# Attention and a gated MLP on one core: the moves of turned probabilities issued on ScalarE's queue instead of SyncE's, with the order of operations rewritten

## The chip, the cores and the metric

One core of one Trainium2 chip runs the whole program. The metric is the time of one execution on the device in microseconds (us), as the median of several runs.

## The reference

Causal attention of 4 batches, 12 heads, 448 positions and head size 64, then a gated MLP over the 1792 tokens of 768 features (12 heads x 64), all in float32:

```python
scores = scale * np.matmul(q, k.transpose(0, 1, 3, 2))
scores = np.where(mask, -1000000000.0, scores)
scores = scores - np.max(scores, axis=-1, keepdims=True)
attn = np.exp(scores)
attn = attn / (np.sum(attn, axis=-1, keepdims=True) + 1e-09)
x = np.matmul(attn, v)               # then (B, H, S, D) -> (B * S, H * D)
gate = 1.0 / (1.0 + np.exp(-(x @ w_gate)))
val = x @ w_val
out = gate * val @ w_out             # 768 -> 1536 -> 768
```

## The kernel before

**The work.** A pair is two heads of one batch; there are 24, six to a batch. A unit is one batch's 448 tokens. Two units go through the MLP one after the other (`unit_items`, then `first_out`); the last two go through it together (`pair_items`) by a scheme of seven products of half-sized blocks. Each product in full precision is three matmuls of rounded halves: high x high, high x low and low x high (`triple` at L756, `mm` at L972). For these, ScalarE makes the high half of a weight tile (L666) and GpSimd or VectorE the low half (L668).

**The weights.** They arrive as words of 64 bits. A load (L642, issued by SyncE) brings a tile into the buffer `room`; ScalarE (L646) and VectorE (L648, L650) convert it to float32. A `keep` (L656) writes it to the chip's memory, and later fetches (L660) bring it back.

**Attention.** Pairs 0 to 5 are done first, in narrow steps. Pairs 6 to 23 run "wide", between about 60 and 390 us, spread among the MLP's products. For a wide pair SyncE loads the raw operands (L358, L363) and V (L369). TensorE computes the scores (L475) and VectorE adds the mask and takes the extremes (L498). ScalarE takes exponentials with their sums (L505), VectorE the reciprocals (L514, L516), and GpSimd scales the probabilities (L526). Then `shift` turns the pair. GpSimd clears a corner of the turned buffer (L537), which waits until an earlier pair's moves have read that buffer. VectorE transposes blocks of 32 x 32 in eight instructions (L541, L544). **Four moves** (L550) each copy 32 partitions of the turned buffer, `tb` or from pair 18 on a part of `room`, into one column range of `pt`, so that blocks that lay on four groups of partitions come to lie on one. Each move waits for all eight transposes and the clearing. `wpv` then multiplies with V: a burst of 40 matmul records (L566), which needs all four moves. ScalarE rounds the result (L443) and VectorE takes the rest (L444), as features of the MLP.

**The order.** Every instruction of the program (or small group, as three matmuls, or a burst) is one operation, given to the planner by `plan.op` with its engine, a cost in us and, as `extra`, the time until its result can be used. Operations are numbered in the order of these calls, 0 to 3069. The order in which they are written into the engines' queues is not computed in the kernel: `TABLE` lists all 3070 numbers, and `Plan.order` only asserts that it holds every number once and that no operation stands ahead of one that it depends on. An engine runs its own operations in the order of that list, each waiting for its inputs. A DMA is issued by the engine that it is listed for, in the same queue as that engine's other work. All DMAs of the kernel before are issued by SyncE ("SP" in the plan, "SPq" in the profile).

```python
full = [(tb, "zero", "end", *[(z, i) for z in range(2) for i in range(3)], (0, 3))]
for a in range(4):
    plan.op("SP", dma(32 * 4 * WC * 4), lambda a=a: nc.sync.dma_start(
        out=pt.t[:, a * WC:a * WC + WC], in_=at_()[32 * a:32 * a + 32]), full, [(pt, a)], extra=4.2)
```

Of the kernel before, what the change touches and what calls it, by code (L numbers as in the profile page):

```python
# [40 lines left out]
WC = 512  # L41
# [248 lines left out]
def kernel(  # L290
# [7 lines left out]
    nc = tc.nc  # L298
    plan = Plan()
# [10 lines left out]
    dma = lambda b: b / 355e3 + 0.03  # L310
# [219 lines left out]
    def shift(n):  # L530
# [18 lines left out]
        for a in range(4):  # L549
            plan.op("SP", dma(32 * 4 * WC * 4), lambda a=a: nc.sync.dma_start(  # L550
                out=pt.t[:, a * WC:a * WC + WC], in_=at_()[32 * a:32 * a + 32]), full, [(pt, a)], extra=4.2)
# [705 lines left out]
```

## Time and profile before

| | |
|---|---|
| median of 3 runs | 640.65 us (638.57 to 642.12) |
| the profiled execution | 641.33 us, its span 639.4 us |
| mean granted clock of TensorE | 0.995 |
| busy: TensorE, VectorE, ScalarE, GpSimd | 610.3, 459.6, 335.3, 310.9 us |
| DMA: hardware queue that SyncE issues on | 131.36 MB, 62.4% of 16 engines' span |
| moves at L550 | 48 from `tb`, 24 from `room`: 18 pairs x 4, 256 KB each |

The span runs from the first to the last instruction of one execution; the time of the run also has what lies around it. Busy times are of the engines' instructions; a queue's time in issuing a DMA or in waiting isn't counted as busy. A number in brackets at the end of a timeline row is the engine's idle time before that instruction, with what ended it.

### The profile page before, as it was taken

The page shows a single profiled execution, that of the slowest core. Times are in us where ns is not written, and L with a number is a line of the kernel's source. Part 1 is how long each engine was busy: PE and PEld are TensorE (multiplying, and loading weights), DVE is VectorE, ACT ScalarE, POOL GpSimd, SP SyncE. Part 2 cuts the span into 40 slices and gives each one's busy share as a digit, 9 for nine tenths or more (in the row PEclk, how much of TensorE's full clock was granted, in tenths as well). Part 3 has the DMA queues.
Part 4 walks back from the last instruction along what each step waited for, and adds up shares of the span by engine and source line. Part 5 has one row for each costly group of instructions (what it writes and reads, how often), then busy time and mean ns, then how long its engine had stood idle before and what let it go on. Part 6 is the DMA issues. An engine that isn't in the chain of part 4 may idle for free.

```text
span 639.4 us, 11811 instructions
## 1 busy us (share of the span) xinstructions
PE 610.3 (95%) x4128; PEld 527.2 (82%) x4128; DVE 459.6 (72%) x1109; ACT 335.3 (52%) x760; POOL 310.9 (49%) x349
## 2 busy tenths in 40 slices
PE   7999998989999999999899899999999999999997
PEld 4567887868998788888688698889999999899996
DVE  4879887988786766678868768864546366978862
ACT  6788656645543737556537544643343343465630
POOL 3660323241555666667567784574566557410120
PEclk9999999999999999999899999999999999999999
DMA  6489999998998899994675595222422322424512
GB/s 236 115 321 342 288 353 303 310 310 265 371 304 314 293 316 364 310 332 138 195 208 160 156 278 190 89 78 96 139 75 74 126 74 74 132 90 129 186 46 86
DMA packets 51034, 132.09 MB, mean 207 GB/s; under 512 B 5664, under 2 KB 12320, under 8 KB 50976
## 3 DMA queue, kind: packets, MB, share of 16 engines
q1 hardware_dynamic: 50976, 131.36, 62.4%
q8 instruction: 32, 0.52, 0.3%
q14 instruction: 26, 0.21, 0.1%
HBM read 89.26 MB, written 23.20 MB: 176 GB/s over the span
## 4 chain that ended last, share of the span: by engine, by line
PE 45%; DMA 19%; DVE 16%; ACT 7%; issue 5%; POOL 4%; SPq 3%; DVEq 0%; ACTq 0%; POOLq 0%
PE m L972 18%; PE s L972 10%; PE m L756 7%; PE t L972 5%; DMA room<-in_wp_dram 4%; DMA wr<-wdram 4%; DVE sm L498 3%; DMA sum<-wd 3%; POOL sm L526 2%; ACT sm L505 2%; DMA out_dram<-gt 2%; DMA pt<-room 2%; PE m L566 2%; SPq L550 2%; PE t L401 2%
## 5 line engine op out<-in xcount | busy, mean ns | idle before, releaser
L526 POOL TENSOR_SCALAR sm<-sm,r 128x384 f32<-128x384 f32 (+3 forms) x165 | 96.9, 606 | 105.7 <-DVE r L516 75.8
L756 PE MATMUL m<-xh,wh 128*128 128x448 f32 x342 | 128.6, 376 | 3.6 <-DVE r L514 1.9
L756 PE MATMUL m<-xh,wl 128*128 128x448 f32 x342 | 126.5, 370 | 2.3 <-POOL wl L668 1.7
L756 PE MATMUL m<-xl,wh 128*128 128x448 f32 x342 | 125.6, 367 | 0.0
L944 POOL TENSOR_TENSOR wl<-room,wh 128x384 fp32r<-128x384 f32 x84 | 91.2, 1107 | 64.5 <-ACT wh L943 63.1
L505 ACT ACTIVATE sm<-sm,mn 128x384 f32<-128x384 f32 (+3 forms) x168 | 88.0, 526 | 39.1 <-DVE mn L498 32.0
L668 POOL TENSOR_TENSOR wl<-wr,wh 128x768 fp32r<-128x768 f32 x46 | 88.3, 1924 | 34.6 <-ACT wh L666 34.3
L943 ACT CAST wh<-room 128x384 fp32r<-128x384 f32 x84 | 40.8, 511 | 71.1 <-DVE room L953 25.0
L756 PEld LDWEIGHTS m<-xh,wh 128*128 128x128 f32 x342 | 64.7, 189 | 12.8 <-issue 2.7
L666 ACT CAST wh<-wr 128x768 fp32r<-128x768 f32 x57 | 47.3, 831 | 52.9 <-DMA wr<-wdram 24.6
L756 PEld LDWEIGHTS m<-xh,wl 128*128 128x128 f32 x342 | 64.6, 189 | 9.9 <-POOL wl L668 3.5
L756 PEld LDWEIGHTS m<-xl,wh 128*128 128x128 f32 x342 | 64.8, 190 | 4.9
L541 DVE STREAM_TRANSPOSE tb<-sm 128x384 f32<-128x384 f32 (+2 forms) x84 | 34.9, 442 | 25.6 <-POOL sm L526 20.6
L498 DVE CUSTOM_DVE_ANT_0 sm<-s,mask 128x128 f32<-128x128 f32 (+3 forms) x108 | 41.9, 400 | 8.2 <-PE s L475 8.1
L972 PE MATMUL m<-pt,wh 128*128 128x448 f32 x150 | 44.8, 367 | 1.5 <-DVE xl L725 1.1
L475 PE MATMUL s<-raw 64*64 64x128 f32 (+3 forms) x432 | 40.6, 405 | 5.9 <-DMA raw<-in_qkt_dram 3.6
L566 PEld LDWEIGHTS m<-pt,vr 128*64 128x64 f32 x720 | 34.8, 141 | 12.2 <-issue 8.7
L725 DVE TENSOR_TENSOR xl<-m,xh 128x448 f32<-128x448 f32 x30 | 18.5, 621 | 35.8 <-PE m L972 35.5
L566 PE MATMUL m<-pt,vr 128*64 128x128 f32 (+1 forms) x720 | 37.1, 260 | 5.8 <-DMA pt<-room 3.4
L756 PE MATMUL m<-ob,wh 128*128 128x448 f32 x120 | 35.1, 372 | 2.9 <-DVE ob L735 1.5
L972 PE MATMUL m<-sm,wh 128*128 128x448 f32 x126 | 36.8, 365 | 0.0
L953 DVE TENSOR_TENSOR room<-room 128x384 f32<-128x384 f32 x48 | 30.2, 632 | 7.2 <-POOL wl L944 6.6
(207 smaller groups left out, 1357.0 us busy)
## 6 DMA issues: line engine op xcount, KB each, us to landing
room<-in_wp_dram SPq DMA_DIRECT2D x36, 768.0 KB, 7.4
room<-wdram SPq DMA_DIRECT2D x36, 384.0 KB, 3.6
pt<-tb SPq DMA_DIRECT2D x48, 256.0 KB, 4.9
raw<-in_qkt_dram SPq DMA_DIRECT2D x23, 448.0 KB, 6.9
wr<-wdram SPq DMA_DIRECT2D x24, 384.0 KB, 5.6
sum<-wd SPq DMA_DIRECT2D x21, 384.0 KB, 5.3
wr<-sum SPq DMA_DIRECT2D x21, 384.0 KB, 5.5
room<-sum SPq DMA_DIRECT2D x21, 384.0 KB, 3.7
```

The costliest lines, as they stand in the source:

```text
L475: nc.tensor.matmul(out=sp[z].t[c:c + 64, o:o + ne], lhsT=q, rhs=k)
L498: plan.op("DVE", dve(n), lambda z=z, i=i, sp=sp, sm=sm, n=n, o=o, f=f, lo=lo, to=to, first=first: nc.vector.tensor_tensor_reduce(out=sm.t[ ...
L505: plan.op("ACT", act(ne, 0, 1) + 0.09, lambda z=z, sm=sm, i=i, ne=ne, off=off: nc.scalar.activation(out=sm.t[:, off:off + ne], in_=sm.t[:, ...
L526: plan.op("PL", 0.24 + w / 1200, lambda sm=sm, e=e, o=o, w=w, z=z: nc.gpsimd.tensor_scalar(out=sm.t[:, o:o + w], in0=sm.t[:, o:o + w], sca ...
L541: plan.op("DVE", dve(128 * c) + 0.03, lambda sm=sm, i=i, o=o, c=c, at=at: nc.vector.transpose(out=tv()[:, :, at:at + 32 * c].rearrange("p ...
L566: nc.tensor.matmul(out=vp.t[64 * z:64 * z + 64, i * WQ:i * WQ + rows(i)], lhsT=v.t[:, c, z], rhs=src, start=(c == 0), stop=(c == i))
L666: plan.op("ACT", act(768), lambda: nc.scalar.copy(hi_.t, t.t), [(t,)], [(hi_,)])
L668: plan.op(eng, cost, lambda: at.tensor_tensor(out=lo_.t, in0=t.t, in1=hi_.t.bitcast(F32), op=ALU.subtract), [(t,), (hi_,)], [(lo_,)], lock ...
L756: nc.tensor.matmul(out=ps.t[:, :S], lhsT=a.t[:, kw, :], rhs=b.at, start=bool(start and z == 0), stop=bool(stop and z == 2))
L943: plan.op("ACT", act(w), lambda: nc.scalar.copy(f(hi_.t), x()), [(src, at)], [(hi_, e)])
L944: plan.op("PL", 0.97, lambda: nc.gpsimd.tensor_tensor(out=f(lo_.t), in0=x(), in1=f(hi_.t).bitcast(F32), op=ALU.subtract), [(src, at), (hi_ ...
L972: nc.tensor.matmul(out=ps.t[:, :S], lhsT=a.t[:, kw, :], rhs=b.at, start=bool(first and z == 0), stop=bool(last and z == 2), skip_group_che ...
```

## The change

The four moves of each wide pair are issued by ScalarE, so that they stand in ScalarE's queue among its exponentials, conversions and roundings, and not in SyncE's among loads and stores. In the plan each costs ScalarE 0.5 and its data count as usable 5.5 after that, where 4.2 stood. What moves the bytes, their number and what each move waits for are as before. All of `TABLE` is replaced by another order of the same 3070 numbers. Only the part of it around pair 10 is shown; there 820 is the load of a weight tile (L642) and 821 its conversion on ScalarE (L646), 834 and 835 are another such load and conversion, 692 to 695 are the pair's four moves and 780 is its burst.

```diff
 TABLE = """
...
-    608 617 612 655 677 734 669 735 632 761 678 614 622 679 746 820 656 725 762 747 790 682 726 675 736 727 749 803
-    748 728 1533 791 633 696 623 683 624 670 626 763 634 629 635 686 729 625 1534 627 687 750 630 737 697 701 628
-    699 689 738 636 685 751 702 861 688 704 739 705 723 752 684 690 740 717 804 741 764 753 707 691 718 692 754 698
-    703 805 694 742 693 706 695 755 806 708 862 1541 792 807 700 719 709 793 710 724 794 834 716 756 848 720 721 765
-    795 783 722 743 784 863 711 872 865 780 714 883 808 767 712 768 775 769 713 757 774 821 715 773 796 770 781 785
...
+    653 734 631 607 654 638 609 677 655 618 667 804 791 668 620 621 805 678 622 615 679 792 617 669 735 760 834 725
+    632 614 806 726 656 749 727 623 761 728 696 736 729 762 763 820 750 793 633 682 848 624 683 630 634 860 670 629
+    635 689 626 687 636 737 697 628 702 699 627 701 751 723 706 625 703 752 698 688 708 738 691 835 685 753 686 861
+    684 754 956 821 690 1030 724 739 692 822 740 694 705 741 693 764 695 755 707 823 742 700 756 836 794 891 765 717
+    837 704 783 808 709 784 795 838 807 785 824 718 786 710 809 719 787 713 720 743 862 825 714 721 767 757 769 716
+    772 849 715 722 780 863 773 711 771 712 775 957 774 928 768 796 781 766 770 788 1132 892 797 883 798 867 776 850
...
 """
...
         for a in range(4):
-            plan.op("SP", dma(32 * 4 * WC * 4), lambda a=a: nc.sync.dma_start(
-                out=pt.t[:, a * WC:a * WC + WC], in_=at_()[32 * a:32 * a + 32]), full, [(pt, a)], extra=4.2)
+            plan.op("ACT", 0.5, lambda a=a: nc.scalar.dma_start(
+                out=pt.t[:, a * WC:a * WC + WC], in_=at_()[32 * a:32 * a + 32]), full, [(pt, a)], extra=5.5)
```

## Rows read from the trace of the kernel before

**Rows 1.** The page, busy us (share of the span) and instructions of each engine.

```profile
PE 610.3 (95%) x4128; PEld 527.2 (82%) x4128; DVE 459.6 (72%) x1109; ACT 335.3 (52%) x760; POOL 310.9 (49%) x349
```

**Rows 2.** Stretches: from:to, length, each engine's busy us, TensorE's clock, DMA share, GB/s.

```profile
142.00:145.40 3.40, 3.40 (x16) 2.63 (x16) 3.40 (x13) 1.75 (x5) 3.40 (x7) 0.50 1.01 297
316.10:319.50 3.40, 3.40 (x32) 3.15 (x28) 1.38 (x5) 2.04 (x5) 3.40 (x7) 0.50 0.28 106
...
60.00:280.00 220.00, 212.72 (x1632) 182.46 (x1634) 169.07 (x473) 123.26 (x289) 100.34 (x127) 0.99 0.95 317
280.00:390.00 110.00, 101.47 (x797) 86.92 (x790) 83.57 (x214) 61.23 (x144) 77.05 (x75) 0.98 0.68 210
70.00:390.00 320.00, 304.18 (x2351) 260.79 (x2350) 242.68 (x651) 175.76 (x409) 174.00 (x194) 0.99 0.85 277
0.00:70.00 70.00, 63.26 (x596) 44.83 (x597) 53.83 (x200) 53.49 (x145) 30.96 (x60) 1.00 0.77 266
390.00:639.40 249.40, 242.84 (x1185) 221.59 (x1183) 163.12 (x259) 106.07 (x208) 105.90 (x95) 1.00 0.30 99
```

**Rows 3.** TensorE's waits from 60 to 390 us: us in total, times, longest.

```profile
PE m L566 <- DMA pt<-room: 3.4, 2, 3.0
PE m L756 <- POOL wl L668: 2.1, 7, 0.7
...
PE m L756 <- DVE wl L668: 0.6, 1, 0.6
```

**Rows 4.** Timeline, the starts of five bursts (and one clearing): start us, us, instruction.

```profile
110.54 0.15 POOL L537 MEMSET tb<- 128x64 f32 x1 [1.86 <-issue]
...
110.64 0.40 PE L566 MATMUL m<-pt,vr 128*64 128x128 f32 x3 [1.50 <-issue]
...
127.10 0.44 PE L566 MATMUL m<-pt,vr 128*64 128x128 f32 x4 [0.29 <-DMA pt<-tb]
...
315.17 0.66 PE L566 MATMUL m<-pt,vr 128*64 128x128 f32 x8 [3.00 <-DMA pt<-room]
...
333.37 0.33 PE L566 MATMUL m<-pt,vr 128*64 128x128 f32 x2 [0.44 <-DMA out_dram<-gt]
...
353.38 0.33 PE L566 MATMUL m<-pt,vr 128*64 128x128 f32 x2 [0.35 <-DMA pt<-room]
```

**Rows 5.** Timeline, the last transpose of the pair late at 315 us, and its moves.

```profile
304.22 0.56 DVE L541 STREAM_TRANSPOSE room<-sm 128x384 f32<-128x384 f32 x1
304.85 0.56 SPq L550 DMA_DIRECT2D pt<-room  x1
...
308.35 1.21 SPq L550 DMA_DIRECT2D pt<-room  x2
```

**Rows 6.** Line L550: issue times, ns min/median/max, and time to landing.

```profile
L550 SPq DMA_DIRECT2D pt<-tb x48: 548/606/1645, 70.2 to 275.6; - x48
...
DMA to landing us min/median/max: 3.5/4.9/7.3
```

**Rows 7.** From 60 to 390 us: landings of weight loads (L642), of raw loads (L358).

```profile
DMA to landing us min/median/max: 5.0/7.4/9.6
...
DMA to landing us min/median/max: 4.8/7.1/9.2
```

**Rows 8.** Timeline, a conversion that waits for its load, and what follows it.

```profile
136.87 0.92 ACT L646 ACTIVATE wd<-room 128x768 f32<-128x768 f32 x1 [3.79 <-DMA room<-in_wp_dram]
...
140.81 0.58 DVE L444 TENSOR_TENSOR xl<-m,xh 128x448 fp32r<-128x448 f32 x1
...
141.45 0.47 PE L756 MATMUL m<-xh,wh 128*128 128x448 f32 x1 [1.85 <-DVE r L514]
```

**Rows 9.** Waits of SyncE's queue from 60 to 390 us, the two longest.

```profile
SPq L550 <- DVE tb L541: 25.8, 9, 7.0
SPq L550 <- DVE room L541: 24.1, 3, 13.0
```

**Rows 10.** Waits of ScalarE from 60 to 390 us, the line on loaded weights.

```profile
ACT wd L646 <- DMA room<-in_wp_dram: 11.3, 5, 5.7
```

247 rows, old and new, of the table TABLE are left out of this document.

## The prediction

> **What bounds the kernel now.** I read the page's busy table first: TensorE is busy 610.3 of 639.4 us, the next engine 72% [rows 1]. So a change elsewhere can only return idle time of TensorE, or time at its lower clock. The stretches say where that is [rows 2]: TensorE idles 6.7 us before 70 us, 15.8 us from 70 to 390 us, where pairs are turned by the moves beside the first two units' products, and 6.6 us after it, where nothing is moved. In the middle stretch two stages differ: from 60 to 280 us the 16 DMA engines are 0.95 busy, from 280 to 390 us 0.68. ScalarE is busy 175.8 of the 320 us.
>
> Next, who ended TensorE's waits between 60 and 390 us [rows 3]. A landing of moves is the largest releaser. Five bursts (L566) start late: by 1.50, 0.29, 3.00, 0.44 and 0.35 us [rows 4]. Three rows name a move's landing. At 110.64 us the row says "issue", but GpSimd's clearing of the turned buffer, which waits for the same moves, starts 0.1 us earlier. At 333.37 us an output's landing is named; a burst reads no output, so I count it to the moves as well. Together 5.58 us. The 3.00 us wait is followed, 0.9 us after it ends, by 3.4 us at clock 0.50, the lower of the two levels (1.2 instead of 2.4 GHz), with TensorE busy throughout; that costs half of it, 1.7 us [rows 2].
>
> The queue of the worst burst says why [rows 5]. The pair was turned at 304.78 us. SyncE issued the first move at 304.85 us, but between it and the last two (from 308.35 us) stood four other instructions: a load of operands of scores, the second move, a load of V and a fetch of weights. Four moves in a row would take 4 x 0.606 = 2.4 us [rows 6].
>
> **The change, part by part.** A move lands 4.9 us after its issue in the median (3.5 to 7.3) [rows 6]. What the written order leaves for it I worked out from the two lists: between two entries I add the planner's costs of the TensorE operations listed (0.608 us for three products, 1.95 for a pair's scores, 2.0 for its burst). Before, 4.2 to 5.5 us of such work stand between a pair's last move and its burst in 13 of 18 pairs; in the new list at least 6.0 in all, on average 1.4 us more.
>
> (a) The five waits. The late pairs at 315, 333 and 353 us have 6.1, 6.0 and 8.5 us instead of 5.4, 4.2 and 4.3, and no load of SyncE between their moves. All three go: 3.79 us. The two early ones (1.79 us) lie in the DMA-bound stage; what replaces them there is (c). Taken: -5.6, between 0 and -5.6.
>
> (b) The low clock at 316 us came after the 3.00 us wait and goes with it: -1.7, between 0 and -1.7.
>
> (c) ScalarE's queue keeps its order, so what stands ahead of the moves now delays them. In pairs 6, 7, 9 and 10 of the new list a conversion (L646) of a freshly loaded weight tile stands just ahead, at most one instruction between, and its load (L642) is listed only 4.3, 5.8, 5.8 and 3.6 us of TensorE's work before it. Such a load takes 7.4 us in the median, 5.0 to 9.6 [rows 7]. So the conversion, and the moves behind it, would be 3.1, 1.6, 1.6 and 3.8 us late. The bursts have 6.7, 7.9, 6.1 and 7.4 us after the last move, so 1.8, 3.0, 1.2 and 2.5 us to spare over 4.9: TensorE waits 1.3 + 0 + 0.4 + 1.3 = 3.0 us. With loads of 9.6 us it is 3.5 + 0.8 + 2.6 + 3.5 = 10.4, with 5.0 nothing. Taken: +3.0, the median's. That such a wait reaches TensorE can be seen before: a conversion waited 3.79 us for its load, VectorE's feature split came behind it, and TensorE lost 1.85 us [rows 8].
>
> (d) Issue time on ScalarE: 72 moves x 0.606 = 43.6 us, 2.4 us a pair. Its cover is ScalarE's 320 - 175.8 = 144 us of idle time [rows 2]. Behind the moves stand the next pair's exponentials (L505), for whose sums VectorE waits, and the high halves of weights (L666), on whose low halves TensorE waits through GpSimd or VectorE: 2.1 + 0.6 us before [rows 3]. If the cover is gone, those waits double, +2.7; if the list's longer lead for low halves (at least 1.2 us, was 0) ends them, -2.7. Taken: 0, as the two oppose each other.
>
> (e) SyncE's queue loses 72 issues and its waits for the turns, 25.8 + 24.1 us in 12 waits [rows 9]; ScalarE takes over those it reaches too early. Loads behind them leave sooner, but from 60 to 280 us the engines that carry them are full [rows 2]: 0. Against it, the new list puts one raw load only 7.3 us of TensorE's work ahead of its scores (at least 16.7 before); such loads land after 4.8 to 9.2 us [rows 7], so up to +1.9 there. Taken: 0.
>
> (f) The rewritten order before 70 us and after 390 us moves TensorE's operations by a few places; the idle time there, 6.7 and 6.6 us, may shift by 2 us either way. Taken: 0.
>
> Sum: 641.33 - 5.6 - 1.7 + 3.0 = 637.0 us against the profiled execution (its span 639.4 and 1.9 us around it). That one lies 0.7 us above the median of the three runs, 640.65, so I forecast 636.4.
>
> **The rivals.** *The moves land sooner on a queue of their own.* On SyncE's queue a move stands behind loads of weights; its fastest landing is 3.5 us, the median 4.9 [rows 6]. If a queue apart brings all near 3.5, the spare in (c) grows by 1.4 us to 3.2, 4.4, 2.6 and 3.9, more than every lateness there, and (c) is nothing: 641.33 - 7.3 = 634.0, 633.4 by the median. For it: the spread of landings. Against: with the DMA engines at 0.95, the load that the conversion waits for pays. The Trainium skill, "DMA: Bandwidth & Descriptors", section "Queues, rings and completion order", has each DMA engine take turns between queues packet by packet, which is this case; no run shown has a second queue.
>
> *No gain, as the transfers are what is late.* If the DMA engines and not the queue set the landings, the two early waits stay, only the three late ones and the clock return 5.5 us, and (c) with +3.0 and (d) with +2.7 give it back: 641.5, 640.8 by the median. For it: 0.95 busy in the first stage [rows 2]. Against: the 3.00 us wait lies at 0.68, with SyncE's other issues visibly in between. The same page, section "Issuing engines are not separate DMA queues", says that issuing from several engines saves only the sequencer's time; the trace agrees that the engines are full early, and shows 3.5 us between first and third move in the late stage.
>
> *Slower: ScalarE held by late loads.* The place is again pairs 6, 7, 9 and 10. With loads of 9.2 us the conversions are 4.9, 3.4, 3.4 and 5.6 us late, the bursts 3.1 + 0.4 + 2.2 + 3.1 = 8.8. The two waits of 3.1 us are as long as that which preceded the low clock, so 2 x 1.7 more: 641.33 - 7.3 + 8.8 + 3.4 = 646.2, 645.5 by the median. It decides from loads of some 8.5 us upward, where (c) and one drop of the clock eat the gain. For it: loads up to 9.6 us, in the fullest stage. Against: the median is 7.4, and SyncE, without its waits for turns, may issue them sooner than listed.
>
> **How the numbers follow.** About 0.5% (3.2 us) is what a measurement can tell from no change: faster means below 637.4, slower above 643.9. My forecast gets 0.30, the queue apart 0.20, no gain 0.28, slower 0.22. So faster 0.50, same 0.28, slower 0.22. The forecast's own range is 633.4 to 639. The range for 8 in 10 starts at 630: the queue apart, and also the 1.85 us wait at 141 us gone [rows 8], with the half clock (1.7) that follows it too [rows 2], is 629.9. It ends at 646, just above the slower case.
>
> **What would show it.** Right: no burst at L566 waits over 0.5 us after 280 us; clock 1.00 around 316 us; the moves as four issues on ScalarE's queue with no load between them; SyncE without waits at L550. (c): idle time of ScalarE before L646 on "room<-in_wp_dram" between 60 and 140 us, above the 11.3 us of the whole middle stretch before [rows 10], followed by bursts of pairs 6 and 10 waiting for moves. The queue apart: landings near 3.5 us. No gain: landings as before and new waits at "wl". Wrong altogether: TensorE's idle time from 70 to 390 us at 15.8 us or more.

## The result, and the profile after

The changed kernel takes 648.37 us (median of 4 runs, 645.74 to 650.55) against 640.13 us (638.57 to 642.12) for the kernel before: a ratio of 1.0125 [1.0077, 1.0174]. It is slower, and lies 2.4 us outside the range given. The profiled execution took 650.55 us, its span 648.8, the mean clock is 0.982 (before 0.995).

One thing to read more exactly ahead of the rest: each move takes 32 partitions of 8 KB and spreads them over all 128 partitions of `pt`, 2 KB each, and doesn't just copy them "into one column range".

The page first: the busy table, the clock in 40 slices of 16.2 us, the second queue, the chain by engine, and the bursts' group (its last numbers are TensorE's idle time before it).

```profile
PE 613.0 (94%) x4128; PEld 530.5 (82%) x4128; DVE 466.6 (72%) x1109; ACT 334.8 (52%) x760; POOL 309.2 (48%) x349
...
PEclk9999799799799999989999999999999999999999
...
q1 hardware_dynamic: 40608, 112.48, 49.7%
q10 hardware_dynamic: 10368, 18.88, 11.8%
...
PE 57%; DMA 15%; DVE 8%; ACT 7%; ACTq 6%; issue 3%; POOL 3%; SPq 1%; DVEq 0%; POOLq 0%
...
L566 PE MATMUL m<-pt,vr 128*64 128x128 f32 (+1 forms) x720 | 40.8, 275 | 13.7 <-DMA wr<-wdram 4.7
```

The busy times are those of before [rows 1] within 2%. The moves' 18.88 MB are now a queue of their own, with ScalarE's issuing (ACTq) 6% of the chain. The bursts' idle time is 13.7 us; before it was 5.8, the five waits of [rows 4] and a sixth of 0.23 us at 212.5 us. The clock dips are all in the first half. The stretches have the columns of [rows 2]; the stretch with moves ends some 5 us later than before, so it is cut at 395.

```profile
0.00:70.00 70.00, 61.63 (x604) 43.08 (x604) 58.84 (x208) 54.09 (x143) 30.29 (x60) 1.00 0.84 279
60.00:280.00 220.00, 200.46 (x1489) 171.92 (x1488) 154.25 (x435) 111.35 (x258) 89.53 (x117) 0.95 0.89 301
70.00:395.00 325.00, 303.79 (x2302) 260.96 (x2304) 235.17 (x635) 171.20 (x405) 167.55 (x193) 0.96 0.81 264
395.00:648.80 253.80, 247.60 (x1226) 226.49 (x1222) 172.64 (x266) 109.47 (x213) 111.37 (x97) 1.00 0.32 105
69.60:76.30 6.70, 5.38 (x14) 4.79 (x15) 1.85 (x3) 3.93 (x11) 0.00 (x0) 0.50 0.67 221
113.90:120.70 6.80, 5.75 (x46) 5.46 (x47) 6.77 (x23) 4.22 (x8) 5.13 (x9) 0.50 0.96 321
165.10:171.90 6.80, 5.67 (x46) 5.37 (x47) 2.06 (x10) 1.95 (x6) 2.04 (x4) 0.50 0.98 375
277.80:281.10 3.30, 3.30 (x40) 3.18 (x36) 1.85 (x8) 0.49 (x2) 2.95 (x5) 0.50 0.71 273
```

Four stretches ran at clock 0.50, 23.6 us in all where two of 3.4 were before. Each began during one of TensorE's four longest waits in the stretch with moves, or just after it. In TensorE's timeline (start, duration, in brackets the wait):

```profile
70.92 0.74 PE L756 MATMUL m<-xh,wh 128*128 128x448 f32 x1 [3.57 <-ACT gt L780]
...
114.95 1.34 PE L566 MATMUL m<-pt,vr 128*64 128x128 f32 x10 [3.64 <-issue]
...
166.23 1.12 PE L566 MATMUL m<-pt,vr 128*64 128x128 f32 x8 [4.74 <-DMA wr<-wdram]
...
277.47 0.92 PE L566 MATMUL m<-pt,vr 128*64 128x128 f32 x8 [1.98 <-DMA pt<-tb]
```

Three are bursts, which wait for moves (a burst reads no `wr`; the fetch named ended last by chance). Where the time went follows from counting matmuls: the start of the k-th of the new kernel minus that of the k-th before (amount of work, not the same operation).

```
k (time in the new kernel)    600 (66 us)  700 (82)  1000   1400   1900-2300      2500-2700  end
new minus before, us              -4.6       +1.6    +5.8  +11.1   +13 to +17.2      ~+10     +9.3
```

The new list's opening is 4.6 us ahead; all of the loss falls between 67 us and the middle of the stretch with moves; then some comes back. The sum: bursts' waits 13.7 - 5.8 = +7.9, half clock (20.1 us of busy time in the four stretches against 6.8, each costing half) +6.6, opening -4.6, together +9.9, against 648.8 - 639.4 = 9.4. It is a rough one: the wait for `gt` of 3.57 us and what was gained elsewhere aren't in it.

**What makes the moves late.** The line's own view: issue times in ns (min/median/max), then landings.

```profile
L550 ACTq DMA_DIRECT2D pt<-tb x48: 550/734/3237, 64.6 to 287.9; - x48
...
L550 ACTq DMA_DIRECT2D pt<-room x24: 550/628/2034, 297.4 to 385.2; - x24
...
DMA to landing us min/median/max: 3.6/6.8/10.6
```

The maximum doubled from 1645 ns [rows 6] and the landing's median rose from 4.9 to 6.8 us. Added up, the 72 issues took 75.2 us (57.7 before). ScalarE's timeline shows what this does ("x4" is four issues in a row, their time together).

```profile
64.55 0.92 ACT L646 ACTIVATE wr<-room 128x768 f32<-128x768 f32 x1 [0.46 <-ACT sm L505]
64.57 5.70 ACTq L550 DMA_DIRECT2D pt<-tb  x4
70.32 0.54 ACT L780 ACTIVATE gt<-m 128x448 f32<-128x448 f32 x1 [4.86 <-DVE wd L650]
...
82.89 6.24 ACTq L550 DMA_DIRECT2D pt<-tb  x4
89.18 0.40 ACT L505 ACTIVATE sm<-sm,mn 128x128 f32<-128x128 f32 x1 [5.50 <-DVE mn L498]
...
118.95 0.94 ACT L646 ACTIVATE wr<-room 128x768 f32<-128x768 f32 x1 [1.07 <-DMA room<-in_wp_dram]
...
119.99 5.43 ACTq L550 DMA_DIRECT2D pt<-tb  x4
125.47 0.51 ACT L505 ACTIVATE sm<-sm,mn 128x256 f32<-128x256 f32 x1 [5.15 <-issue]
```

The first instruction behind each four starts 0.05 us after they end (64.57 + 5.70 = 70.27, then 70.32), whatever the bracket names. From 64.57 us on the four take 5.70 us; ScalarE finishes a conversion that it began before them, then stands idle for 4.86 us, and `gt`, which TensorE waits for at 67.35, starts at 70.32. That the queue held it, and not the releaser named, an experiment below shows at the same place. Over the 72 issues ScalarE was busy beside them in 14.0 us, so it was held idle for 61.2 (worked out from the trace; the expectations below have 14.9 and 60.3, which count instructions that overlap each other twice). By their place within a pair's four the issues took on average

```
                          1st    2nd    3rd    4th
SyncE, before             0.57   0.78   0.95   0.90 us
ScalarE, after            0.56   0.78   1.31   1.54 us
```

so it is the later ones, with earlier moves still under way, that grow.

The three late bursts have another cause: the moves land later. They belong to pairs 8, 11 and 16. From the end of the turn to the last landing these took 13.4, 12.7 and 12.6 us; with the same list and the moves on SyncE (the first run below) 11.6, 9.7 and 9.5 us. The turns themselves weren't late: between turn and burst TensorE had 9.9, 8.3 and 10.8 us of work, there 10.3, 8.3 and 10.0. Pair 11, with the longest wait, shows it best. In both runs its four issues stand in a row, and they take less time on ScalarE. Its issues and landings, with the change and then in that run:

```profile
153.25 2.71 ACTq L550 DMA_DIRECT2D pt<-tb  x4
DMA to landing us min/median/max: 8.0/8.8/10.6
...
141.38 3.31 SPq L550 DMA_DIRECT2D pt<-tb  x4
DMA to landing us min/median/max: 6.7/6.8/6.9
...
150.56 0.66 PE L566 MATMUL m<-pt,vr 128*64 128x128 f32 x8 [1.75 <-DVE gh L784]
```

There TensorE waited 1.75 us for the burst, here 4.74. Over the 18 pairs the fourth move is issued 3.2 us after the first (4.6 us in that run), and the move that lands last does so 7.7 us after its issue (5.5 us). So the slow issues aren't what makes the sets late.

### The profile page after: what moved, and what is told of

Its sections match the earlier page's. It is cut to its first block, busy times and chain, and to the rows that moved or that the text cites. A ratio compares the mean times of both kernels' runs of the same rounds, so it can differ in the third digit from the quotient of the medians.

```text
span 648.8 us, 11780 instructions
## 1 busy us (share of the span) xinstructions
PE 613.0 (94%) x4128; PEld 530.5 (82%) x4128; DVE 466.6 (72%) x1109; ACT 334.8 (52%) x760; POOL 309.2 (48%) x349
## 3 DMA queue, kind: packets, MB, share of 16 engines
q10 hardware_dynamic: 10368, 18.88, 11.8%
## 4 chain that ended last, share of the span: by engine, by line
PE 57%; DMA 15%; DVE 8%; ACT 7%; ACTq 6%; issue 3%; POOL 3%; SPq 1%; DVEq 0%; POOLq 0%
PE m L972 18%; PE m L756 14%; PE s L972 10%; DMA room<-in_wp_dram 7%; PE t L972 6%; ACTq L550 6%; PE m L566 3%; ACT sm L505 3%; DMA pt<-tb 2%; PE s L475 2%; DMA out_dram<-gt 2%; DMA wr<-wdram 1%; ACT wh L666 1%; DMA raw<-in_qkt_dram 1%; POOL wl L668 1%
## 5 line engine op out<-in xcount | busy, mean ns | idle before, releaser
L526 POOL TENSOR_SCALAR sm<-sm,r 128x384 f32<-128x384 f32 (+3 forms) x165 | 93.7, 588 | 96.0 <-DVE r L516 65.0
L756 PE MATMUL m<-xh,wh 128*128 128x448 f32 x342 | 130.0, 380 | 4.5 <-ACT gt L780 3.6
L756 PE MATMUL m<-xl,wh 128*128 128x448 f32 x342 | 127.2, 372 | 2.0 <-POOL xl L732 1.1
L505 ACT ACTIVATE sm<-sm,mn 128x256 f32<-128x256 f32 (+3 forms) x168 | 88.0, 525 | 56.9 <-DVE mn L498 35.4
L668 POOL TENSOR_TENSOR wl<-wr,wh 128x768 fp32r<-128x768 f32 x46 | 86.3, 1880 | 57.6 <-ACT wh L666 52.9
L756 PEld LDWEIGHTS m<-xh,wh 128*128 128x128 f32 x342 | 65.6, 192 | 13.4 <-ACT gt L780 4.3
L566 PEld LDWEIGHTS m<-pt,vr 128*64 128x64 f32 x720 | 38.4, 151 | 20.0 <-issue 10.0
L566 PE MATMUL m<-pt,vr 128*64 128x128 f32 (+1 forms) x720 | 40.8, 275 | 13.7 <-DMA wr<-wdram 4.7
L475 PE MATMUL s<-raw 64*64 64x128 f32 (+3 forms) x432 | 38.6, 392 | 4.6 <-DMA raw<-in_qkt_dram 3.0
L953 DVE TENSOR_TENSOR room<-room 128x384 f32<-128x384 f32 x48 | 33.6, 702 | 5.8 <-POOL wl L944 5.3
```

What stands on the lines that cost most here:

```text
L475: nc.tensor.matmul(out=sp[z].t[c:c + 64, o:o + ne], lhsT=q, rhs=k)
L505: plan.op("ACT", act(ne, 0, 1) + 0.09, lambda z=z, sm=sm, i=i, ne=ne, off=off: nc.scalar.activation(out=sm.t[:, off:off + ne], in_=sm.t[:, ...
L526: plan.op("PL", 0.24 + w / 1200, lambda sm=sm, e=e, o=o, w=w, z=z: nc.gpsimd.tensor_scalar(out=sm.t[:, o:o + w], in0=sm.t[:, o:o + w], sca ...
L566: nc.tensor.matmul(out=vp.t[64 * z:64 * z + 64, i * WQ:i * WQ + rows(i)], lhsT=v.t[:, c, z], rhs=src, start=(c == 0), stop=(c == i))
L668: plan.op(eng, cost, lambda: at.tensor_tensor(out=lo_.t, in0=t.t, in1=hi_.t.bitcast(F32), op=ALU.subtract), [(t,), (hi_,)], [(lo_,)], lock ...
L756: nc.tensor.matmul(out=ps.t[:, :S], lhsT=a.t[:, kw, :], rhs=b.at, start=bool(start and z == 0), stop=bool(stop and z == 2))
```

## The experiments

Two theories first. A: the queue costs the time (ScalarE is held by its issues). B: the new order does. Each ratio is against runs of the kernel before on the same chip.

**Undo the queue alone: the new list, moves on SyncE.**

```diff
-nc.scalar.dma_start(out=pt.t[:, a * WC:a * WC + WC], ...
+nc.sync.dma_start(out=pt.t[:, a * WC:a * WC + WC], ...
```

> The new list kept, the four moves issued by SyncE again at the same places of the list. If the queue of the moves costs the time (theory A: ScalarE is held while it issues, 75.2 us for 72 moves against 57.7 us on SyncE, and the moves land 6.8 us after issue in the median against 4.9), the time falls to 640 us or below, landings return to about 5 us, and the waits of TensorE for moves (13.7 us before L566) fall below 6 us. If the rewritten order costs it (theory B), it stays within 3 us of 648 us and the first stage still loses some 10 us.

Measured: 636.77 against 639.25 us, 0.9952 [0.9915, 0.9989]. The line's view, and the opening (columns as above):

```profile
L550 SPq DMA_DIRECT2D pt<-tb x48: 542/862/1951, 65.2 to 268.4; - x48
...
DMA to landing us min/median/max: 3.6/5.2/9.2
```

```profile
0.00:70.00 70.00, 63.84 (x614) 45.22 (x615) 58.17 (x208) 56.93 (x153) 30.18 (x60) 1.00 0.82 275
```

614 matmuls are started by 70 us, 596 before [rows 2]: the opening belongs to the list. The median issue is longer than on ScalarE and the landing later than before, and the kernel is still not slower. B falls.

**The queue alone: the old list, moves on ScalarE.** The same edit the other way, on the kernel before.

> The old list, with only the engine of the four moves changed to ScalarE. Theory A: slower than 640 us by 5 us or more, with issues on ScalarE near 1.0 us each and landings near 7 us. Theory B: 638 to 643 us, since the order that cost the time is not there.

Measured: 654.5 against 639.25 us, 1.0228 [1.0179, 1.0277]. The issues took 67.6 us, of which 42 held ScalarE idle, and the bursts' idle time is 18.1 us. So the queue costs the time, with either list, and less with the new one. Whether it does so by the hold, as A has it, is the next question.

**The hold without the queue.** Two theories on how the queue costs it: A1, ScalarE is held by the issues; A2, the moves land later. New list, moves on SyncE; at the moves' places in ScalarE's order stand copies into a scratch tile, which wait for the turn as the moves did. Two or one for each move in later runs.

```diff
+def move(a):
+    nc.sync.dma_start(out=pt.t[:, a * WC:a * WC + WC], in_=at_()[32 * a:32 * a + 32])
+    for _ in range(3):
+        nc.scalar.copy(idle.t, at_()[:, :300])
```

> The new list, the moves issued by SyncE, but at each move's place ScalarE runs three copies of 300 columns into a scratch tile, some 1.05 us, after the same transposes. This leaves ScalarE held as in the changed kernel and gives the moves their old queue. If the hold of ScalarE is most of the cost (theory A1), 645 us or more; if the later landing is (theory A2), within 2 us of the run with the moves on SyncE and no copies.

Measured: 668.18 against 639.25 us, 1.0448 [1.0401, 1.0496]. 216 copies of 442 ns hold ScalarE for 95.5 us; landings are as with SyncE alone (5.2 us), yet TensorE's idle time between 60 and 420 us, apart from bursts, is 28.7 us (12.3 with the change), and the low clock lasts 30.7 us. Three copies were more than the change's own hold, so the dose was cut.

> The new list, moves issued by SyncE, and at each move's place two copies of 300 columns on ScalarE, some 60 us in all. That is what ScalarE lost in the changed kernel: of 75.2 us of issuing it was busy beside it in 14.9, so 60.3 us are idle. Theory A1 (ScalarE held is the cost): 645 to 655 us, near the changed kernel's 648. Theory A2 (landing is the cost): within 3 us of 637 us.

```profile
L556 ACT CAST idle<-tb x96: 427/442/447, 65.2 to 275.5; 128x300 bf16<-128x300 f32 x96
L556 ACT CAST idle<-room x48: 427/443/447, 284.4 to 377.9; 128x300 bf16<-128x300 f32 x48
```

Measured: 646.97 against 641.38 us, 1.0119 [1.0072, 1.0166]. 144 x 0.442 = 63.6 us of hold, about the change's 61.2, with landings at 5.2 us, cost as much in all as the change (1.0125).

> As the run with two copies, with one copy of 300 columns a move, some 30 us in all. Theory A1: between 637 and the time with two copies, about 640 to 645 us. Theory A2: within 2 us of 637 us.

Measured: 635.36 against 641.38 us, 0.9888 [0.9835, 0.9941], for 31.7 us. The doses side by side, with TensorE's idle time and its busy time at half clock from 60 to 420 us of the profiled execution (for the change 20.3 us at half clock; the four stretches cut above hold 20.1):

```
                hold us   ratio    idle: bursts   other   busy at half clock
list alone         0      0.995         8.4        10.5          6.7
one copy          31.7    0.989         7.4        13.0          5.7
two copies        63.6    1.012         9.8        15.9         10.0
three copies      95.5    1.045         6.5        28.7         29.1
the change        61.2    1.0125       13.7        12.3         20.3
```

The first 30 us of copies cost nothing that can be measured; behind that each 32 us costs 15 to 21 us. The 144 us of idle time weren't the cover; some 30 us were. So a hold alone can cost as much as the change did. But the last row shows that the change's loss isn't that of two copies: the copies lose outside the bursts, the change at the bursts and at half clock. That the two ratios agree is in part chance, and how much of the change's cost is the hold's isn't shown.

**Every second move on the other queue**, by column block (an even block on ScalarE, an odd one on SyncE).

```diff
-nc.scalar.dma_start(
+(nc.sync if a % 2 else nc.scalar).dma_start(
```

> The new list, two of the four moves issued by ScalarE and two by SyncE. Theory A: between the changed kernel's 648 us and the run with all four on SyncE, about the middle if both parts of the cost go with the number of moves. Theory B: 648 us as before.

Measured: 636.05 against 639.25 us, 0.9961 [0.9923, 0.9998]. ScalarE's issues take 30.0 us, 10.2 of them beside its work, so it is held for 19.8. A single move still lands after 6.7 us, so that alone need not cost anything. But a pair's set takes 9.9 us from its first issue to its last landing (10.9 with the change, 10.1 with the list alone), and the bursts' idle time is 6.0 us. The hold and the set both shrank here, so this run doesn't tell them apart.

**Spread the four.** Only the list is changed: a pair's third and fourth moves are set behind the second and fourth next ScalarE operations, so that work stands between.

> The changed kernel with the third and fourth move of each pair set behind the second and fourth of ScalarE's next operations in the list, so that ScalarE works while the first two moves drain; the bytes, the queue and the number of issues stay. Theory A1: the idle time behind the moves falls and the time with it, to 645 us or below. Theory A2: no better than 648 us, since the last moves are issued no sooner and the bursts have less time left.

```profile
L550 ACTq DMA_DIRECT2D pt<-tb x48: 550/561/2581, 65.0 to 281.2; - x48
...
L550 ACTq DMA_DIRECT2D pt<-room x24: 550/551/2030, 289.3 to 377.3; - x24
...
DMA to landing us min/median/max: 3.6/6.2/10.1
```

Measured: 642.39 against 641.38 us, 1.0015 [0.9981, 1.0049]. The issues shrink to 57.8 us, 35.1 of them beside ScalarE's work, so 22.7 us are held, and the time is back at that of before. It doesn't go below, as the last moves are now issued later, a set takes 11.3 us and the bursts wait 16.3 us. This run parts the two: the hold fell, the sets did not get faster, and 1.1% came back, so the hold has its share. In the profiled executions most of that is half clock, 6.5 us of busy time for 20.3.

**Two moves on each queue**, those listed first on ScalarE, the last two on SyncE.

```diff
-nc.scalar.dma_start(
+(nc.scalar if a in FRONT[n - WIDE] else nc.sync).dma_start(
```

> The new list, the first two moves of each pair in the list issued by ScalarE and the last two by SyncE. In the changed kernel the first two issues took about 0.6 us each and the last two 1.0 to 3.2 us. Theory A1: ScalarE is held less than 25 us in all, and the time is that of the moves on SyncE, 637 us, or a little better. Theory A2: between 637 and 648 us as far as landings stay at the changed kernel's 6.8 us.

Measured: 635.31 against 641.38 us, 0.9869 [0.9802, 0.9937]. Held: 31.6 - 9.6 = 22.0 us; the four are issued sooner as a set, so from the first issue to the last landing a pair takes 9.9 us (10.9 with the change) though the single landing stays at 6.7. The bursts' idle time is 5.6 us, the low clock 3.4 us. It was run again, more often.

> The run with the first two moves on ScalarE and the last two on SyncE once more, with more rounds: a ratio of 0.98 to 0.995 to the kernel before, that is 629 to 638 us, if its first measurement holds.

```profile
60.00:390.00 330.00, 316.96 (x2427) 275.04 (x2426) 260.40 (x688) 184.88 (x429) 179.70 (x206) 0.99 0.83 277
```

```profile
64.51 0.92 ACT L647 ACTIVATE wr<-room 128x768 f32<-128x768 f32 x1 [0.94 <-ACT sm L506]
64.53 1.49 ACTq L551 DMA_DIRECT2D pt<-tb  x2
66.07 0.55 ACT L781 ACTIVATE gt<-m 128x448 f32<-128x448 f32 x1 [0.65 <-DVE mn L499]
```

Measured: 632.16 against 639.43 us, 0.9875 [0.9824, 0.9926]: a version that beats both kernels. The first fence is its stretch, the second ScalarE's timeline at the place shown above: behind two issues instead of four `gt` starts at 66.07 us, after 0.65 us of idle time and not 4.86. How much of the gain is the split's own isn't shown: with one copy a move and all moves on SyncE, the same list took 635.36 us, on the chip on which the split took 635.31.

**The split without the list: the old list, two moves on each queue.** Is the split enough?

> The old list with the first two moves of each pair on ScalarE and the last two on SyncE. If the split by itself brings the gain (theory D1), 638 us or below. If the rewritten list with its longer leads brings it (theory D2), 640 us or above, as the old list leaves 4.2 to 5.5 us from last move to burst and has no room on ScalarE.

Measured: 642.12 against 639.43 us, 1.0022 [0.998, 1.0064]. No gain: the split needs the list. Whether it is the list's longer way from moves to burst or its better opening wasn't tested apart. The list alone gave 0.9952 [0.9915, 0.9989], whose interval overlaps that of list and split.

**Why the later issues take long: half the bytes.** The changed kernel, each move carrying 256 of its 512 columns; GpSimd fills the other half with zeros, so half of the turned probabilities is left out of the product.

```diff
+nc.gpsimd.memset(pt.t[:, a * WC + WC // 2:a * WC + WC], 0.0)
 nc.scalar.dma_start(
-    out=pt.t[:, a * WC:a * WC + WC], in_=at_()[32 * a:32 * a + 32])
+    out=pt.t[:, a * WC:a * WC + WC // 2], in_=tv()[32 * a:32 * a + 32, :, :WC // 2])
```

> The changed kernel with each move carrying the first 256 of its 512 columns; the other half of the turned probabilities is left out (GpSimd fills it with zeros, some 20 us of its time in all). Issues, waits and places stay. If the issues are held because the earlier moves have not drained (theory C1), the third and fourth issue fall from 1.3 and 1.5 us to below 0.9, ScalarE's idle time in issuing from 60 us to about 30, and the time to 641 us or below. If a later issue on ScalarE costs its time whatever it carries (theory C2), they stay above 1.2 us and the time near 648 us.

```profile
L552 ACTq DMA_DIRECT2D pt<-tb x48: 550/617/1771, 63.6 to 260.4; - x48
...
L552 ACTq DMA_DIRECT2D pt<-room x24: 550/614/1197, 269.5 to 354.6; - x24
...
DMA to landing us min/median/max: 2.5/4.7/7.9
```

Measured: 621.86 against 639.43 us, 0.9723 [0.966, 0.9787]. By place the issues take 0.56, 0.69, 0.79 and 0.61 us: the third and fourth, 1.31 and 1.54 with all bytes, shrink to nearly the first's. So the bytes that earlier moves have still to carry hold an issue. Bytes of its queue under way aren't all of it: with the new list and all moves on SyncE, 19 moves were issued with over 2 MB of that queue not yet landed, loads above all, and took 0.84 us on average. ScalarE is held for 47.6 - 13.4 = 34.2 us, about what the copies had free. The ratio itself mixes this with the faster landing (4.7 for 6.8 us) and 9.4 MB less traffic (DMA share 0.75 from 60 to 390 us, 0.86 before), so it isn't the price of the hold.

## Why the prediction was wrong

**Two steps failed: (d), and the landing of 4.9 us on which (a) and (c) count.** (d) priced the 72 issues at 0.606 us, the median of a skewed row (548/606/1645 [rows 6]), 43.6 us, and covered them with 144 us of idle time of ScalarE [rows 2]. Neither held. Already before, on SyncE, the issues took 57.7 us in all: the maximum in the row said that some were long, and long issues come last in the four, when they stand in a row. With no load between them they took 75.2 us, 61.2 of it with ScalarE idle. And the idle time is no store: the work that counts stands right behind a pair's moves, the next pair's exponentials and the gate's `gt`. The first `gt` of the stretch, held for 4.86 us, cost TensorE 3.57 us, and a stretch at half clock began in that wait. The doses show that 30 us of hold go free and that 64 us can cost as much as the whole change.

The other step has no letter. The prediction kept the landing of before, 4.9 us in the median, for the new queue, and gave the bursts their spare over it. It was 6.8 us (5.2 with the same list on SyncE), and for the move that lands last 7.7 (5.5). That, and not the hold, kept the bursts of pairs 8, 11 and 16 waiting, 10.4 of the bursts' 13.7 us (3.3 with the list alone), with three of the four stretches at half clock. The queue as a whole, hold and landing, cost some 11 us, 0.9952 (list alone) against 1.0125, where (d) had 0 (±2.7) and the landing nothing. How the 11 us divide stays open.

**(a)** was right where the room lies late: from 281 us on no burst waits over 0.5 us but one of 1.43 us at 393.69, just behind the last moves. The early 1.79 us that (a) counted as gone became 3.64 + 4.74 + 1.98 us and two below 1 us, 11.8 in all, as the sets landed late. The prediction's sign of being wrong altogether came true: from 70 to 395 us TensorE is idle for 21.2 us.

**(b)** The low clock at 316 us went, and the clock is 1.00 from 281 us on; but 23.6 us of it came earlier, behind the new waits. The price per stretch (half of the busy time) was right; their number wasn't.

**(c)** had the early stage right, and the wrong pairs and mechanism. Of the bursts of pairs 6, 7, 9 and 10 only the last waited, 0.51 us. Conversions waited for their loads only twice among the four pairs, 1.07 and 0.61 us, and in all four the first move was issued within 0.4 us of the end of the turn. The moves weren't held by what stands ahead; what stands behind them was held, and they landed late.

**(e)** As said, no gain: SyncE no longer waits at L550, and waits for buffers instead, as this row of its waits (us in total, times, longest) says of the fetches of weights (10.7 us before):

```profile
SPq L660 <- POOL wl L668: 65.9, 28, 8.4
```

**(f)** The opening, taken as 0 ± 2, gained 4.6 us.

**The rivals.** The slower one was right in sign, in the early stage, in half clocks behind long waits and nearly in time (645.5 for 648.4). It was wrong in its pairs and its cause, so the time is luck. The moves' own queue went the other way: the landing's median rose to 6.8 us instead of falling to 3.5. Each DMA engine takes turns between queues, a packet at a time (the Trainium skill, "DMA: Bandwidth & Descriptors", section "Queues, rings and completion order"). That fits, as moves would now share with loads that SyncE issues behind them; no run tested it apart. The no-gain rival said that the transfers are what is late, and in part they were. It quoted the section "Issuing engines are not separate DMA queues" of that page of the Trainium skill: only the sequencer's time is saved. The traces add the other half: here the time was moved, 75.2 us of it, onto an engine that had other work.

**Open:** how the queue's cost divides into hold and late landing; why moves land later on ScalarE's queue, why those on SyncE did too when every second one was on ScalarE (6.7 us), and why some sets of the early stage landed 12 to 13 us after their first issue; why an issue is held by moves under way and less by loads; and what the half-byte run owes to the lighter traffic.

## What to carry to other kernels

A DMA issue put on a compute engine is work of that engine: price a whole row of issues by its sum and its maximum, not the median of one, and look at what stands right behind it, not at the engine's idle share. Don't carry a landing time over to another queue: ask by how much it may grow, and what then waits. If the bytes of two such transfers are still under way when the third is issued, try two on each of two queues. Undo each half of a change with two parts: here the list was worth -0.5% and the queue some +1.7%. And when a run that imitates a cause costs as much as the change, look whether it costs it at the same places.

## What the runs showed of the hardware

An issue's time isn't constant: on ScalarE's queue four moves of 256 KB in a row took 0.56, 0.78, 1.31 and 1.54 us on average (3.24 at most), with half the bytes 0.56, 0.69, 0.79 and 0.61. While issues last, an instruction begun before them runs on beside them (64.55 and 64.57 us); at the three places shown the first one behind starts 0.05 us after their end. A queue of their own made the moves land later, not sooner: 6.8 us in the median, 5.2 with the same list on SyncE's queue and 4.9 before.
